# Attention score products of a head pair pinned into an alternating order, upper head first

## The chip, the core and the metric

The kernel runs on one core of one Trainium2 chip. The metric is the device time of one execution in microseconds; the kernel before takes 839.2 us as the median of 3 runs (838.42 to 839.84).

## What is computed

The reference chains three layers over 4 batches of 768 tokens with 8 heads of 48 channels (3072 tokens of 384 channels in all):

```python
state = alpha[:, :, t, :, None] * state + np.einsum('bhd,bhe->bhde', k[:, :, t], v[:, :, t])
y[:, :, t] = np.einsum('bhd,bhde->bhe', q[:, :, t], state)      # gated linear attention
...
h = x @ w_in                                                     # 384 -> 2048
y = (h * (1.0 / (1.0 + np.exp(-h)))) @ w_out                     # 2048 -> 384
...
expert_idx = np.argmax(logits, axis=1)                           # 8 experts, one per token
out[mask] = gate_w[mask, None] * (np.maximum(x[mask] @ w1[e], 0.0) @ w2[e])
```

## The kernel before, in words

**Attention** is done in 24 chunks of 128 tokens (`NCH`; chunk n is tokens c of batch b with c, b = divmod(n, 4)). A chunk handles 8 heads as 4 pairs: a head's 48 channels are padded to 64, so that the lower head of a pair lies on partitions 0 to 63 and the upper one on 64 to 127. The steps of a chunk are written as small functions: `att_A` transposes the decays on TensorE (`transpose4`, L619) and scans them on VectorE (L627), which gives the factors P and R (L632, L634); `att_Bk` and `att_Bq` transpose keys and queries and multiply the factors in (L649, L674); `att_C` (L685 to L702) makes the score products; `att_S` splits the masked scores into two 16-bit parts (L710, L711); `att_KT` scales the keys in place on GpSimd (L724), splits them and sends them through a transposing DMA (L729); `att_D` makes the output y (L758, L765) and splits it (L506); `att_U` multiplies keys and values (L799) and updates the state (L808, L813).

**The score products** are 8 per chunk: for each of 4 pairs p and each head i of it, a 128x128 block of keys times queries in 32-bit floats that contracts the 64 partitions of that head alone. Each product of 32-bit floats appears in the trace as two matmul records and two weight loads, so a chunk has 16 records of L692. The products of the lower heads go to the PSUM bank `sc0`, those of the upper heads to `sc1`. Each bank is copied out as a whole by ScalarE (L697), masked by GpSimd (L698) and used by `att_D`.

**PSUM banks.** `bank` (L390) gives out banks. In the first part of the program they come from all eight; once the blocks run (`turn[0] = None`), every bank that attention asks for, and those of `route`, come from one pool of three (`ps_a`). `att_C` asks for `sc0` first and for `sc1` second, so a score product waits for the reader of whatever lay in its bank before.

**The first feed-forward layer** runs in 8 blocks of 384 tokens: `mm1` (L870, 9 matmuls of 128x384 into `hp`) then SiLU on ScalarE and a split (L877 to L879), and `mm2` (L893, 9 matmuls of 128x392 into three accumulators). While block j runs, the steps of the attention chunks for block j+2 are pumped in between (`pump_j`), and weights of the experts are loaded and split (`pump_w`). At the end of a block `finish` pumps what is missing, and `route` picks the expert of each token and scatters its row. After the last block come `expert1` (L1183) and `expert2` (L1209), tile by tile, to the end.

**What sets the order.** The program is built with a scheduler that plays the instructions through a timeline of its own and fixes the order on each engine by when an instruction is ready there; the order of the source is a wish, not a rule. On the chip each engine then follows that fixed order. `behind` (L480) adds an edge between two instructions of one engine for that scheduler: the one is placed behind the other, without a semaphore between them.

Of the kernel before, what the change touches and what calls it, by code (L numbers as in the profile page):

```python
# [272 lines left out]
def attention_silu_moe_kernel(  # L273
# [14 lines left out]
    nc = tc.nc  # L288
# [83 lines left out]
    if True:  # L372
# [17 lines left out]
        def bank(dims, dtype, name):  # L390
            at = (ps_a, "at")
            wide = [at, at, at, (ps_o, "o0"), (ps_o, "o1"), (ps_o, "o2"), (ps_h, "h"), (ps_h, "h")]
            pool, tag = at if turn[0] is None else wide[turn[0] % 8]
            if turn[0] is not None:
                turn[0] += 1
            return pool.tile(dims, dtype, tag=tag, name=name)
# [83 lines left out]
        def behind(ins, before):  # L480
            tc.add_manual_dep(
                ins.ins, before.ins.name, mybir.DependencyInfo(mybir.DependencyClass.NoSync, mybir.DependencyReason.DATA),
                reason="the first block's tokens come before the weights that it uses last",
            )

        def from64(raw, f, gate=None, first=None):
            r = raw.rearrange("p (n w) -> p n w", w=2)
            lo, hi = r[:, :, 0], r[:, :, 1]
            fi = f.bitcast(I32)
            ins = nc.vector.tensor_scalar(  # L490
                out=fi, in0=hi, scalar1=3, scalar2=0x3FFFFFF8, op0=ALU.logical_shift_left, op1=ALU.bitwise_and
            )
            if gate is not None:
                after(ins, gate)
            if first is not None:
                behind(ins, first)
            nc.vector.scalar_tensor_tensor(
                out=fi, in0=lo, scalar=29, in1=fi, op0=ALU.logical_shift_right, op1=ALU.bitwise_or
            )
            nc.vector.scalar_tensor_tensor(  # L500
                out=fi, in0=hi, scalar=-0x40000000, in1=fi, op0=ALU.bitwise_and, op1=ALU.bitwise_or
            )
# [72 lines left out]
        def load_w1(c, e):  # L575
            st = work[:, F * (e % 2):F * (e % 2 + 1)]
            nc.sync.dma_start(out=st, in_=w1[e, c * 128:(c + 1) * 128, :])
            behind(split(st, SW1, w1s["h"][c][:, e, :], w1s["l"][c][:, e, :]), lead["g"])
            if c == 0:
                nc.vector.tensor_reduce(  # L580
                    out=guard("w1", 2.0 ** -6), in_=st[:, 0:64], axis=AXX, op=ALU.max, apply_absolute_value=True
                )
# [102 lines left out]
        def att_C(n):  # L685
            d = ch[n]
            d["S"] = []
            sc = [bank([128, NPAIR, 128], FP32, f"sc{i}") for i in range(2)]
            for p in range(NPAIR):
                for i in range(2):  # L690
                    r = slice(64 * i, 64 * i + 64)
                    nc.tensor.matmul(  # L692
                        out=sc[i][:, p, :], lhsT=d["K"][r, p, :], rhs=d["Q"][r, p, :], start=True, stop=True
                    )
            for i in range(2):
                s = a2.tile([128, NPAIR, 128], FP32, tag="S", name="S")
                nc.scalar.activation(out=s, in_=sc[i], func=ACTF.Copy, scale=SST if n >= NF else SST * SV)  # L697
                nc.gpsimd.affine_select(  # L698
                    out=s, in_=s, pattern=[[0, NPAIR], [1, 128]], compare_op=ALU.is_ge, fill=0.0, base=0,
                    channel_multiplier=-1,  # L700
                )
                d["S"].append(s)  # L702
# [118 lines left out]
        def att_steps():  # L821
# [10 lines left out]
            for n in range(NCH):  # L832
                more = n + 1 < NCH
                if more:
                    att_A(n + 1)
                    att_load(n + 3, "a")
                yield
                att_C(n)
                yield
                att_S(n)  # L840
# [130 lines left out]
        def weights_a():  # L971
            for c in range(2):
                for e in range(E):
                    load_w1(c, e)
                    yield
# [20 lines left out]
        weights = [weights_a()]  # L996
# [318 lines left out]
        last = lambda t: route(NCH - TPB + t, acc[t])  # L1315
# [91 lines left out]
```

## Time and profile before

| what | value |
|---|---|
| median of 3 runs | 839.2 us |
| the profiled execution | 834.05 us |
| its span, and the mean granted TensorE clock | 832.4 us, 0.974 |
| TensorE busy | 779.0 us, 94% of the span |
| VectorE, ScalarE, GpSimd busy | 500.0, 431.4, 248.2 us |
| score products L692, busy with overlaps counted once | 54.8 us in 384 records |

The profile shows one execution. Its own time, 834.05 us, is 1.65 us more than the span from the first to the last instruction, and 5.15 us less than the median of the runs. "Busy" counts time in which at least one instruction of the group runs, so records that overlap are counted once. The slices divide the span into 40 parts of 20.8 us each.

### The profile page before, as it was taken

The page shows a single profiled execution, that of the slowest core. Times are in us where ns is not written, and L with a number is a line of the kernel's source. Part 1 is how long each engine was busy: PE and PEld are TensorE (multiplying, and loading weights), DVE is VectorE, ACT ScalarE, POOL GpSimd, SP SyncE. Part 2 cuts the span into 40 slices and gives each one's busy share as a digit, 9 for nine tenths or more (in the row PEclk, how much of TensorE's full clock was granted, in tenths as well). Part 3 has the DMA queues.
Part 4 walks back from the last instruction along what each step waited for, and adds up shares of the span by engine and source line. Part 5 has one row for each costly group of instructions (what it writes and reads, how often), then busy time and mean ns, then how long its engine had stood idle before and what let it go on. Part 6 is the DMA issues. An engine that isn't in the chain of part 4 may idle for free. (4 is left out here: it accounts for less than half of the span.)

```text
span 832.4 us, 16583 instructions
## 1 busy us (share of the span) xinstructions
PE 779.0 (94%) x5488; PEld 492.0 (59%) x5488; DVE 500.0 (60%) x1444; ACT 431.4 (52%) x931; POOL 248.2 (30%) x335
## 2 busy tenths in 40 slices
PE   6879799999999999998999988989799999999996
PEld 5756577667667666665657655555344555555553
DVE  7799963767777977786677576466543222222221
ACT  2456664656675846666556575667542222222221
POOL 3342311534453554444222121131343111111111
PEclk9959899999999999999999999999999999999998
DMA  9997132144445454534521345345588666555663
GB/s 188 256 289 201 48 49 48 50 93 80 96 106 118 89 147 100 112 96 86 106 79 47 97 135 159 90 134 153 166 160 188 115 112 121 103 118 120 109 117 61
DMA packets 244028, 98.66 MB, mean 119 GB/s; under 512 B 224969, under 2 KB 233326, under 8 KB 243808
## 3 DMA queue, kind: packets, MB, share of 16 engines
q1 hardware_dynamic: 240288, 86.31, 48.8%
q0 software_dynamic: 3648, 11.18, 3.9%
q8 instruction: 51, 0.84, 0.4%
q14 instruction: 41, 0.34, 0.1%
HBM read 58.40 MB, written 12.36 MB: 85 GB/s over the span
## 5 line engine op out<-in xcount | busy, mean ns | idle before, releaser
L870 PE MATMUL hp<-w2h,wi_h 128*128 128x384 f16 x576 | 146.2, 331 | 7.4 <-ACT w2l L877 5.3
L893 PE MATMUL o<-wo_h,w2l 128*128 128x392 f16 x528 | 147.1, 333 | 6.0 <-DVE wo_h L569 3.6
L1190 DVE SCALAR_TENSOR_TENSOR work<-hp,work 128x512 f16<-128x512 f32 x58 | 39.9, 690 | 121.6 <-ACT work L1189 121.5
L893 PEld LDWEIGHTS <-w2l 128*128 128x128 f16 x792 | 75.5, 98 | 57.9 <-issue 6.9
L870 PEld LDWEIGHTS <-wi_h 128*128 128x128 f16 x768 | 74.0, 98 | 54.7 <-issue 10.1
L1183 PE MATMUL hp<-w1h,xT 128*128 x348 | 103.5, 379 | 2.4 <-DVE work L1190 2.4
L870 PE MATMUL hp<-w2h,wi_l 128*128 128x384 f16 x288 | 94.8, 330 | 0.1
L893 PE MATMUL o<-wo_l,w2l 128*128 128x392 f16 x264 | 87.8, 332 | 0.0
L1183 PEld LDWEIGHTS <-xT 128*128 128x128 f16 x522 | 50.9, 98 | 60.7 <-issue 3.0
L1220 POOL DMA_INDIRECT out_dram<-ob,mt x29 | 28.3, 976 | 176.3 <-ACT ob L1217 171.7
L1189 ACT ACTIVATE work<-hp 128x512 f16<-128x512 f32 x58 | 34.4, 595 | 68.4 <-PE hp L1183 61.6
L893 PE MATMUL o<-wo_h,g 128*128 128x392 f16 x240 | 67.0, 329 | 1.2 <-DVE g L879 1.1
L879 DVE SCALAR_TENSOR_TENSOR w2l<-w2l 128x384 f16<-128x384 f32 x88 | 51.1, 583 | 27.8 <-ACT w2l L878 27.5
L1183 PE MATMUL hp<-w1l,xT 128*128 x174 | 66.0, 379 | 0.0
L877 ACT ACTIVATE w2l<-hp 128x384 f32<-128x384 f32 x88 | 42.4, 483 | 36.0 <-PE hp L870 31.8
L692 PE MATMUL sc<-Q,K 64*128 64x128 f32 x384 | 54.8, 307 | 1.7 <-DVE state L817 1.0
L692 PEld LDWEIGHTS sc<-Q,K 64*128 64x128 f32 x384 | 46.0, 207 | 14.0 <-issue 7.1
L870 PEld LDWEIGHTS <-wi_l 128*128 128x128 f16 x384 | 37.8, 99 | 24.3 <-issue 1.0
L698 POOL TENSOR_SCALAR_AFFINE_SELECT S<-S 128x512 f32<-128x512 f32 x48 | 36.5, 764 | 45.7 <-ACT S L697 45.3
L878 ACT ACTIVATE w2l<-w2l 128x384 f16<-128x384 f32 x88 | 45.7, 521 | 5.8 <-PE o L893 4.1
L870 PE MATMUL hp<-w2l,wi_h 128*128 128x384 f16 x192 | 48.2, 326 | 0.0
L893 PEld LDWEIGHTS <-g 128*128 128x128 f16 x360 | 34.0, 98 | 23.2 <-DVE g L879 2.2
(276 smaller groups left out, 1603.7 us busy)
## 6 DMA issues: line engine op xcount, KB each, us to landing
work<-in_moe_w_dram SPq DMA_DIRECT2D x24, 512.0 KB, 3.8
work<-in_moe_w_dram SPq DMA_DIRECT2D x30, 384.0 KB, 3.5
w1h<-in_moe_w_in_dram SPq DMA_DIRECT2D x6, 768.0 KB, 5.4
nat_a<-in_alpha_dram SPq DMA_DIRECT2D x23, 192.0 KB, 3.2
nat_k<-in_k_dram SPq DMA_DIRECT2D x23, 192.0 KB, 2.8
nat_q<-in_q_dram SPq DMA_DIRECT2D x23, 192.0 KB, 3.2
nat_v<-in_v_dram SPq DMA_DIRECT2D x23, 192.0 KB, 2.9
w1h<-in_moe_w_out_dram SPq DMA_DIRECT2D x5, 768.0 KB, 7.2
```

Source lines behind the costliest of these rows:

```text
L692: nc.tensor.matmul(out=sc[i][:, p, :], lhsT=d["K"][r, p, :], rhs=d["Q"][r, p, :], start=True, stop=True)
L698: nc.gpsimd.affine_select(out=s, in_=s, pattern=[[0, NPAIR], [1, 128]], compare_op=ALU.is_ge, fill=0.0, base=0, channel_multiplier=-1,)
L870: ins = nc.tensor.matmul(out=hp, lhsT=wi[a][f // 2][:, c, (f % 2) * 128:(f % 2 + 1) * 128], rhs=x[:, c, :], start=(n == 0), stop=(n == 3 * ...
L877: nc.scalar.activation(out=g, in_=hp, func=ACTF.Silu, scale=1.0 / (SX * SWI))
L878: nc.scalar.activation(out=gh, in_=g, func=ACTF.Copy, scale=SG)
L879: lead["g"] = nc.vector.scalar_tensor_tensor(out=gl, in0=g, scalar=SG, in1=gh, op0=ALU.mult, op1=ALU.subtract)
L893: nc.tensor.matmul(out=acc[t], lhsT=a[:, ts], rhs=wo[w][f // 2][:, f % 2, :], start=(f == 0 and n == 0), stop=(f == KF - 1 and n == 2),)
L1183: nc.tensor.matmul(out=hp, lhsT=xT[:, a, :], rhs=w1s[w][c][:, bass.ds(d["e"], 1), fs], start=(n == 0), stop=(n == 3 * KD - 1),)
L1189: nc.scalar.activation(out=hs[:, 0], in_=hp, func=ACTF.Relu)
L1190: nc.vector.scalar_tensor_tensor(out=hs[:, 1], in0=hp, scalar=0.0, in1=hs[:, 0], op0=ALU.max, op1=ALU.subtract)
L1220: nc.gpsimd.indirect_dma_start(out=out[:, :], out_offset=bass.IndirectOffsetOnAxis(ap=d["row"], axis=0), in_=ob, in_offset=None, bounds_ch ...
```

## The change

In `att_C` the loop over the two heads is turned round (upper head first), and every score product but the first of a chunk is put behind the one before it with `behind`. The text of the reason in `behind` changes with no effect. Nothing else does: the same products, banks, copies and DMAs.

```diff
             d["S"] = []
             sc = [bank([128, NPAIR, 128], FP32, f"sc{i}") for i in range(2)]
+            prev = None
             for p in range(NPAIR):
-                for i in range(2):
+                for i in (1, 0):
                     r = slice(64 * i, 64 * i + 64)
-                    nc.tensor.matmul(
+                    ins = nc.tensor.matmul(
                         out=sc[i][:, p, :], lhsT=d["K"][r, p, :], rhs=d["Q"][r, p, :], start=True, stop=True
                     )
+                    if prev is not None:
+                        behind(ins, prev)
+                    prev = ins
```

## Rows read from the trace of the kernel before

**Rows 1.** The page: busy time by engine, then TensorE and its clock in 40 slices

```profile
PE 779.0 (94%) x5488; PEld 492.0 (59%) x5488; DVE 500.0 (60%) x1444; ACT 431.4 (52%) x931; POOL 248.2 (30%) x335
...
PE   6879799999999999998999988989799999999996
...
PEclk9959899999999999999999999999999999999998
```

**Rows 2.** Busy time in stretches: length, each engine (instructions), clock, DMA share, GB/s

```profile
42.00:62.00 20.00, 15.35 (x91) 11.04 (x91) 19.38 (x43) 11.93 (x21) 9.15 (x7) 0.50 1.14 285
...
83.00:104.00 21.00, 16.34 (x116) 11.37 (x114) 20.20 (x39) 13.11 (x25) 8.03 (x7) 0.84 0.17 48
...
104.00:464.00 360.00, 353.07 (x2991) 241.78 (x2989) 263.07 (x761) 224.74 (x493) 140.50 (x194) 1.00 0.40 87
464.00:832.00 368.00, 343.31 (x1951) 186.88 (x1948) 144.51 (x479) 152.27 (x341) 68.98 (x83) 0.99 0.58 128
```

**Rows 3.** The same for the score products' line L692 alone: TensorE and weight loads

```profile
5.00:62.00 57.00, 8.89 (x64) 7.63 (x64) 0.79 1.15 257
62.00:104.00 42.00, 3.20 (x16) 2.75 (x16) 0.92 0.47 128
104.00:464.00 360.00, 42.76 (x304) 35.68 (x304) 1.00 0.40 87
```

**Rows 4.** Timeline of TensorE around one chunk: start, length, what, xcount

```profile
258.02 0.49 PE L870 MATMUL hp<-w2l,wi_h 128*128 128x384 f16 x2
258.44 1.16 PE L692 MATMUL sc<-Q,K 64*128 64x128 f32 x8
259.53 0.34 PE L870 MATMUL hp<-w2l,wi_l 128*128 128x384 f16 x1
259.70 0.49 PE L870 MATMUL hp<-w2l,wi_h 128*128 128x384 f16 x2
260.12 1.16 PE L692 MATMUL sc<-Q,K 64*128 64x128 f32 x8
261.21 0.34 PE L870 MATMUL hp<-w2l,wi_l 128*128 128x384 f16 x1
261.38 0.49 PE L870 MATMUL hp<-w2l,wi_h 128*128 128x384 f16 x2
```

**Rows 5.** Timeline of TensorE around the last chunk's score products

```profile
461.43 1.16 PE L692 MATMUL sc<-Q,K 64*128 64x128 f32 x16
462.53 0.34 PE L893 MATMUL o<-wo_h,w2l 128*128 128x392 f16 x1
```

**Rows 6.** Timeline of TensorE around a chunk that follows a route, 228 to 233 us

```profile
228.32 1.16 PE L692 MATMUL sc<-Q,K 64*128 64x128 f32 x8
229.40 0.34 PE L893 MATMUL o<-wo_l,w2l 128*128 128x392 f16 x1
...
230.74 0.49 PE L870 MATMUL hp<-w2l,wi_h 128*128 128x384 f16 x2
231.16 1.16 PE L692 MATMUL sc<-Q,K 64*128 64x128 f32 x8
```

**Rows 7.** Timeline of VectorE ahead of the chunk of rows 4

```profile
257.56 0.53 DVE L506 SCALAR_TENSOR_TENSOR ys<-yp,ys 128x384 f16<-128x384 f32 x1
258.02 0.08 DVE L506 DVE_READ_ACCUMULATOR ys<-yp,ys 128x1 f32 x1
```

**Rows 8.** Waits of TensorE, 62 to 464 us: in total, times, longest

```profile
PE up L799 <- DMA KT<-kd: 4.8, 4, 2.6
...
PE sc L692 <- DVE state L817: 1.0, 1, 1.0
```

**Rows 9.** Line L697, the copies of the scores, 104 to 464 us

```profile
L697 ACT ACTIVATE S<-sc x38: 572/578/598, 116.9 to 463.1; 128x512 f32<-128x512 f32 x38
...
PE sc L692: 7.3, 11
```

**Rows 10.** Line L724, keys scaled in place, 104 to 464 us

```profile
L724 POOL TENSOR_TENSOR K<-K,pend x14: 1037/1041/1529, 161.8 to 391.9; 128x512 f32<-128x512 f32 x14
...
PE sc L692: 2.1, 5
```

**Rows 11.** Timeline of ScalarE around the chunk of rows 4

```profile
260.03 0.58 ACT L697 ACTIVATE S<-sc 128x512 f32<-128x512 f32 x1
...
262.36 0.57 ACT L697 ACTIVATE S<-sc 128x512 f32<-128x512 f32 x1
```

More of the change, by code (lines that the diff above doesn't have):

```diff
@@ L482, in behind @@
                 ins.ins, before.ins.name, mybir.DependencyInfo(mybir.DependencyClass.NoSync, mybir.DependencyReason.DATA),
-                reason="the first block's tokens come before the weights that it uses last",
+                reason="an order within one engine",
             )
```

## The prediction

> **What bounds the kernel now.** I read the page first: TensorE is busy 94% of the span, VectorE 60%, and from the sixth of the 40 slices on nearly every slice of TensorE is full, at the full granted clock [rows 1]. Then the busy time by stretch [rows 2]: from 104 to 464 us, where the feed-forward blocks run with attention pumped in between, TensorE is busy 353.07 of 360 us, VectorE 263.07, ScalarE 224.74, GpSimd 140.50. From 464 us on it is busy 343.31 of 368. Before 104 us it is different: from 42 to 62 us VectorE is busy 19.38 of 20, from 83 to 104 us 20.20 of 21, with TensorE at 15.35 and 16.34. So work taken off TensorE counts in full between 104 and 464 us and hardly at all before.
>
> Next, where the score products stand [rows 3]: 304 of the 384 records of L692 lie between 104 and 464 us, that is 19 of the 24 chunks at 16 records each, and take 42.76 us there.
>
> Then how they stand [rows 4, 5]. In a typical chunk TensorE does 8 records of L692 in 1.16 us, three matmuls of the feed-forward layer, and 8 more records in another 1.16 us. In the last chunk it does all 16 records in the same 1.16 us. The work is equal; the order is not. A product uses 64 of the 128 rows, so two that stand next to each other and use different rows run at the same time; the 16 records in 1.16 us show that. Where one head's four products stand together, they use the same rows and run one after another. That 42.76 = 18 x 2.31 + 1.16 fits 18 chunks of the split kind and one of the paired kind.
>
> **Why they are split.** The loop of before already alternates the heads, but the scheduler places each product when its bank is free. `sc0` is asked for before `sc1`, and both come from the pool of three, so the lower heads' bank comes free first in the scheduler's timeline; it issues those four, fills in with feed-forward matmuls, and issues the four of the upper heads when theirs is free. In chunks behind a route more is filled in [rows 6]: the second run starts at 231.16, 2.84 us after the first. I take the second run to be the upper heads' from the order of the requests; the rows don't name the head.
>
> **The change, part by part.**
>
> *The pinned order.* The first product is now one of the upper heads, whose bank is free last. When it may go, the other seven may go too, and they stand in alternating order. So each of the 18 split chunks should look like the last one.
>
> The cost of a split run: from its start to the start of the next matmul is 259.53 - 258.44 = 1.09 us [rows 4]. It also starts late: of the two matmuls at 259.70, which take 0.49 us together at 0.326 each, the second starts 0.163 later, and one more of them would start at 260.03; the run starts at 260.12, which is 0.09 late. Together 1.18 us a run, 2.36 us a chunk. The paired run costs 462.53 - 461.43 = 1.10 us [rows 5] and one late start, 1.19 us. The difference is 1.17 us a chunk, and 18 x 1.17 = **21.1 us** off TensorE, all of it in the stretch where it is full.
>
> *Upper head first.* Costed at nothing in itself: the work is equal.
>
> *The first part of the program.* The other five chunks' 80 records lie before 104 us and take 8.89 + 3.20 us [rows 3], two of the five in runs that could be shortened further. I cost that at nothing, since VectorE's work is what hides it there (19.38 of 20 and 20.20 of 21 us) [rows 2]. If that cover were gone, pairing would give at most half of what lies there for those two, some 3 us, and that is on the gain's side.
>
> *The added wait.* The lower heads' four products used to go while the upper heads' bank was still held; now all eight stand behind that bank. On TensorE everything placed behind them is queued there, and ScalarE's copies of `sc0` come later by the time between the two runs. Both copies are needed before `att_D` can finish, and the later one isn't later than now, so nobody further on waits longer. What the wait costs TensorE is not in the trace, since it has no such order; bounds: nothing, if the scheduler puts other matmuls in front and the bank is free on the chip when they are done; at most 1.09 us a chunk, the length of the run that used to lie under it, 19.6 us in all. Below nothing it can't be, the wait being new. The rows near it: the split of y that releases a bank of the chunk before ends at 258.10 [rows 7], 0.34 us ahead of the start of even the first run at 258.44 [rows 4]; and a score product is named as having waited for VectorE's state update once in that stretch, for 1.0 us [rows 8]. These lie at the low end, so I take 1.0 us in all.
>
> *Next in line.* With TensorE's 353.07 us down to some 332, VectorE's 263.07 is still 69 us below it, so no other engine becomes the bound on average.
>
> **The sum** against the profiled execution: 834.05 - 21.1 + 1.0 = 813.95 us. The median of the runs shown is 839.2, which is 5.15 us above that execution; I carry the saving over in microseconds: 839.2 - 21.1 + 1.0 = **819 us**.
>
> **A rule that speaks against it.** ScalarE copies each of a chunk's two score banks in 0.578 us, and waited for L692 only 7.3 us over 19 chunks [rows 9]; today the two copies start 2.33 us apart [rows 11]. After the change both banks are full at once and the copies stand one behind the other for 2 x 0.578 = 1.16 us, as long as the paired run itself. The Trainium skill, "TensorEngine Tiling (Array Packing)", section "PSUM Bottleneck", says that packing speeds up the array but not the emptying of PSUM, which can become the bottleneck. By that rule alone nothing would be gained; it makes the second rival below.
>
> **The rivals.**
>
> *The cover is only half replaced.* The scheduler finds too few ready matmuls to place in front of the pinned eight, and TensorE waits for half of the 1.09 us in each chunk: 18 x 0.55 = 9.8 us, which gives 839.2 - 21.1 + 9.8 = 828 us. For it: the first run did lie under the wait. Against it: from the first run's end to the second's start, 0.59 us [rows 4] to 1.76 us [rows 6] of feed-forward matmuls are found to fill in today.
>
> *The copies take over.* If TensorE had to stand for the two copies in each chunk, 18 x 1.16 = 20.9 us come back: 839 us. For it: three banks are few, and two of them are held until copied. Against: ScalarE is busy 224.74 of 360 us [rows 2], and TensorE has feed-forward matmuls to do meanwhile. The same time, 839, results if the change doesn't do what it says, because the scheduler places feed-forward matmuls between the pinned products and so breaks the pairs: an order isn't a neighbourhood.
>
> *Slower: the transposed keys come late.* The in-place scaling of the keys waits for the last score product of the chunk [rows 10], and behind it lie a split, the transposing DMA and then TensorE's L799. TensorE waited for that DMA in 4 of 14 chunks, 4.8 us in all, 2.6 at most [rows 8]. If the new order puts L799 closer behind the scores, this grows. It decides the sign when the 14 waits exceed 21.1 + 4.8 = 25.9 us, 1.85 us each. At 2.6 us in each of the 14: 36.4 - 4.8 = 31.6 us more, 839.2 - 21.1 + 31.6 = 850 us. Against: the chain starts when the scores end, and they end no later than the upper run does now.
>
> **How the numbers follow.** About 0.2%, 1.7 us, is what a measurement of this kernel can tell from no change. The forecast, with the saving kept but for a few microseconds either way (814 to 824 us), 0.78; half replaced, 828 us, 0.12; copies or broken pairs, 839 us, 0.06; late keys, 850 us, 0.04. The range of 8 in 10 is 814 to 829: below, the full 21.1 us with the 3 us of the first part and 1 us of scatter; above, the first rival. Left out are the last two, and a share of the scatter. Faster: 0.78 + 0.12 = 0.90; no difference 0.06; slower 0.04.
>
> **What would show it.** Right: in the timeline of TensorE each chunk after 104 us has one run of 16 records of L692 in about 1.16 us; L692 is busy some 22 us for 304 records where it was 42.76; TensorE's busy time falls by about 21 us, and the stretch from the first route to the last score product by as much; waits of L692 stay at a microsecond or two. The cover is gone if the waits of TensorE name L692 with about 10 us. The copies have taken over if waits name ScalarE's L697. Pairs are broken if L692 still takes over 30 us. The keys come late if the wait for the KT DMA is 20 us or more. The forecast is wrong altogether if L692 is down to 22 us and the time isn't down: then TensorE wasn't what set the end.

## The result and the profile after

The kernel with the change takes 828.98 us as the median of 4 runs (826.74 to 830.09), against 839.52 us (838.42 to 841.26) for the kernel before on the same chip. The ratio is 0.9869, with a 95% interval from 0.9842 to 0.9896: 10.5 us less, and between 8.7 and 13.3. Faster, as forecast; but the forecast was 819 us, and the measured time lies at the very edge of its range of 814 to 829 us, near the time of the first rival.

The page of the kernel after, busy time by engine, then TensorE and its clock in 40 slices (the lines that answer to [rows 1]):

```profile
PE 764.8 (92%) x5488; PEld 476.2 (58%) x5488; DVE 501.3 (61%) x1444; ACT 427.7 (52%) x931; POOL 250.1 (30%) x335
...
PE   6778699999999999999999998999699999999996
...
PEclk9559799999999999999999999999999999999999
```

TensorE is busy 14.2 us less, the other engines as before to within 4 us. Its slices are still nearly all full from the sixth on. The profiled execution after took 828.59 us, near its median; the one before, 834.05, lies some 5 us under its own, so the two traces together show only 5.5 us of the 10.5 (e9 says more on this). Stretches are therefore compared below by what TensorE did in them, not by when they began.

Busy time by stretch, kernel after, columns as in [rows 2]:

```profile
42.00:62.00 20.00, 14.15 (x89) 10.66 (x90) 19.52 (x45) 13.42 (x23) 8.38 (x8) 0.59 1.10 278
83.00:104.00 21.00, 14.19 (x101) 8.87 (x100) 19.09 (x39) 10.90 (x20) 9.03 (x7) 0.76 0.22 57
104.00:464.00 360.00, 350.96 (x3072) 235.28 (x3071) 267.32 (x768) 227.14 (x502) 142.90 (x196) 1.00 0.41 89
```

From 104 to 464 us TensorE idles 360 - 350.96 = 9.0 us where it idled 6.9 [rows 2], and fits more instructions in. Now the score products there, from the view that groups instructions by line (count, busy time, mean ns of one, idle time before):

```profile
L693 PE MATMUL sc<-Q,K 64*128 64x128 f32 x304 | 30.7, 291 | 0.1
```

The same 304 records take 30.7 us where they took 42.76 [rows 3]: **12.1 us off TensorE**, and not the 21.1 of the forecast. The timeline of TensorE around one chunk says why; it answers to [rows 4]:

```profile
262.41 0.33 PE L897 MATMUL o<-wo_l,g 128*128 128x392 f16 x1
262.67 0.49 PE L693 MATMUL sc<-Q,K 64*128 64x128 f32 x2
263.09 0.34 PE L897 MATMUL o<-wo_h,g 128*128 128x392 f16 x1
263.27 0.49 PE L874 MATMUL hp<-w2l,wi_h 128*128 128x384 f16 x2
263.59 0.33 PE L874 MATMUL hp<-w2l,wi_l 128*128 128x384 f16 x1
...
264.24 0.49 PE L874 MATMUL hp<-w2l,wi_h 128*128 128x384 f16 x2
264.66 1.16 PE L693 MATMUL sc<-Q,K 64*128 64x128 f32 x14
265.75 0.34 PE L874 MATMUL hp<-w2l,wi_l 128*128 128x384 f16 x1
```

The chunk has not one run of 16 records but a run of 2 and a run of 14. The first product, by the pinned order the upper head's of pair 0, goes by itself; feed-forward matmuls follow for 1.6 us; then come the other seven, three pairs and one left over. The same two runs stand in all 18 chunks that were split between 104 and 464 us. The lone product costs 263.09 - 262.67 = 0.42 us, the run of 14 costs 265.75 - 264.66 = 1.09, each with a late start of about 0.09 us, worked out as in the prediction: 1.69 us a chunk, where it was 2.36. That is 0.67 us less, and 18 x 0.67 = 12.1 us, the number of the grouped line.

Who waits, kernel after, 104 to 464 us (total, times, longest), first for TensorE, as [rows 8], then for GpSimd:

```profile
PE up L803 <- DMA KT<-kd: 4.7, 5, 1.5
PE o L897 <- DVE w2l L883: 1.7, 3, 0.8
...
POOL K L728 <- PE sc L693: 21.0, 11, 3.2
```

TensorE waits for the transposed keys as long as before (4.7 us against 4.8). GpSimd waits 21.0 us for the last score product before it scales the keys, where it waited 2.1 [rows 10]. In the chunk shown the scaling now stands ahead of both masks (L728 at 265.90 us, L702 from 266.89), where a mask came first before (L698 at 260.69, L724 at 261.36). GpSimd has the room for that, busy 142.90 of 360 us, and TensorE's own idle time grew by 2.1 us in all.

### The profile page after: what moved, and what is told of

The parts are those of the page before. It is cut to its first block, busy times and chain, and to the rows that moved or that the text cites. A ratio compares the mean times of both kernels' runs of the same rounds, so it can differ in the third digit from the quotient of the medians.

```text
span 827.0 us, 16596 instructions
## 1 busy us (share of the span) xinstructions
PE 764.8 (92%) x5488; PEld 476.2 (58%) x5488; DVE 501.3 (61%) x1444; ACT 427.7 (52%) x931; POOL 250.1 (30%) x335
## 5 line engine op out<-in xcount | busy, mean ns | idle before, releaser
L882 ACT ACTIVATE w2l<-w2l 128x384 f16<-128x384 f32 x88 | 45.6, 520 | 4.3 <-PE o L897 2.9
L1213 PEld LDWEIGHTS <-work 128*128 128x128 f16 x336 | 32.9, 98 | 23.3
L1221 ACT ACTIVATE ob<-po,s 128x384 f32<-128x384 f32 x29 | 16.8, 580 | 55.2 <-PE po L1213 35.9
L702 POOL TENSOR_SCALAR_AFFINE_SELECT S<-S 128x512 f32<-128x512 f32 x48 | 31.7, 682 | 44.9 <-ACT S L701 42.2
```

The costliest lines, as they stand in the source:

```text
L702: nc.gpsimd.affine_select(out=s, in_=s, pattern=[[0, NPAIR], [1, 128]], compare_op=ALU.is_ge, fill=0.0, base=0, channel_multiplier=-1,)
L882: nc.scalar.activation(out=gh, in_=g, func=ACTF.Copy, scale=SG)
L1213: nc.tensor.matmul(out=po, lhsT=hT[c // 4][:, (a + c % 4) * 128:(a + c % 4 + 1) * 128], rhs=w2s[w][c][:, bass.ds(d["e"], 1), :], start=(n ...
L1221: nc.scalar.activation(out=ob, in_=po, func=ACTF.Copy, scale=d["fac"], accum_out=guard("finite", 0.0, ALU.not_equal))
```

## The experiments

Every run is compared with runs of the kernel before on the same chip; the column "before, same chip" has their median. The groups ran on different chips, so medians of different groups are better compared by their ratios. "Scores" is the busy time of the score products from 104 to 464 us in the grouped view (for 288 records where it says so, since the last chunk then lies behind 464 us), "idle" is 360 us less the busy time of TensorE in that stretch; both from one profiled execution each.

| kernel | median us | before, same chip | ratio to before, 95% interval | scores us | idle us |
|---|---|---|---|---|---|
| before | 839.52 | 839.52 | 1 | 42.8 | 6.9 |
| after | 828.98 | 839.52 | 0.9869 (0.9842 to 0.9896) | 30.7 | 9.0 |
| e1 lower head first | 833.52 | 838.67 | 0.9941 (0.9909 to 0.9972) | 30.7 | 11.5 |
| e2 turned, unpinned | 843.51 | 838.67 | 1.0070 (1.0044 to 1.0096) | 41.6 (288) | 8.3 |
| e3 both banks | 831.05 | 838.67 | 0.9922 (0.9892 to 0.9953) | 21.4 (288) | 17.7 |
| e4 late only | 826.99 | 838.67 | 0.9873 (0.9843 to 0.9902) | 31.4 | 8.2 |
| e5 unpaired run | 836.35 | 839.92 | 0.9951 (0.9927 to 0.9976) | 30.7 (288) | 13.1 |
| e6 both, late | 831.38 | 839.92 | 0.9898 (0.9861 to 0.9935) | 22.1 (288) | 17.1 |
| e7 turned copies | 847.71 | 839.92 | 1.0092 (1.0058 to 1.0126) | 40.4 (280) | 10.8 |
| e8 held up | 839.94 | 839.92 | 0.9996 (0.9970 to 1.0021) | 23.0 (288) | 18.2 |
| e10 both, VectorE copy | 831.96 | 839.57 | 0.9928 (0.9900 to 0.9956) | 21.4 (288) | 19.4 |
| e11 late, VectorE copy | 839.49 | 839.57 | 1.0006 (0.9985 to 1.0026) | 29.7 (288) | 16.6 |
| e12 fewer pairs | 832.07 | 837.76 | 0.9907 (0.9874 to 0.9940) | 32.6 | 8.7 |

### Which head goes alone, and why: e1 and e2

e1 keeps the pins and puts the lower head first:

```diff
-                for i in (1, 0):
+                for i in (0, 1):
```

> Theory A (a bank of the pool of three goes to whichever product is placed first, so the first product of a chunk, of whichever head, goes alone, and the other seven wait for the second bank): head order doesn't matter. Lower head first with the same pins gives runs of 2 and 14 records again, L692's group busy about 31 us between 104 and 464 us, and the time of the changed kernel, 829 us within 2. Rival B (upper head first is what makes the pairing, since the upper bank is the late one): with the lower head first the gain shrinks or goes, 834 us or more.

TensorE, timeline of one chunk of e1:

```profile
259.94 0.48 PE L693 MATMUL sc<-Q,K 64*128 64x128 f32 x2
260.36 0.34 PE L874 MATMUL hp<-w2l,wi_h 128*128 128x384 f16 x1
...
261.93 1.16 PE L693 MATMUL sc<-Q,K 64*128 64x128 f32 x14
```

The runs are 2 and 14 again, and the scores take the same 30.7 us. So it isn't the upper heads' bank that is late: whichever product is placed first gets the bank that is free first. Theory A is right on the shape. On the time it is off: 833.5 us where 827 to 831 were expected, and a ratio of 0.9941 whose interval lies above that of the change. The score products can't be what differs, since they cost the same. TensorE's idle time is 2.5 us higher (11.5 against 9.0); what else of the new order makes up its distance to the change (4.5 us by the medians, 6 by the ratios) was not settled. So of the change's 10.5 us it isn't shown how much is the pairing's: e1 has the same saving on the score products and gains 5.1 us.

e2 turns the loop and takes the pins out:

```diff
-            prev = None
...
-                    if prev is not None:
-                        behind(ins, prev)
-                    prev = ins
```

> The loop turned round (upper head first) but nothing pinned. Theory A: the scheduler splits the heads as before, now the upper head's four products first: two runs of 8 records, busy 42.8 us between 104 and 464 us, 839.5 us within 2. Rival B (the order of the heads does it): runs of 16 or of 2 and 14 records, 829 us.

TensorE, timeline of one chunk of e2:

```profile
269.23 1.16 PE L692 MATMUL sc<-Q,K 64*128 64x128 f32 x8
270.32 0.34 PE L893 MATMUL o<-wo_h,w2l 128*128 128x392 f16 x1
270.50 0.49 PE L870 MATMUL hp<-w2l,wi_h 128*128 128x384 f16 x2
270.92 1.16 PE L692 MATMUL sc<-Q,K 64*128 64x128 f32 x8
```

Two runs of 8, as in the kernel before: the pins pair the products, not the turning, so Theory A holds on the shape. But the time is 843.5 us, 4.8 us above that of the kernel before on its chip and outside what was expected. ScalarE's timeline of this chunk shows one thing that the turning did:

```profile
272.92 1.06 ACT L697 ACTIVATE S<-sc 128x512 f32<-128x512 f32 x2
```

Both copies come together behind the second run, where they came 2.33 us apart [rows 11], although the first bank is full 1.7 us earlier. e7 tests that.

e7 is e2 with the copies turned as well:

```diff
-            for i in range(2):
+            for i in (1, 0):
                 s = a2.tile([128, NPAIR, 128], FP32, tag="S", name="S")
...
-                d["S"].append(s)
+                d["S"].insert(0, s)
```

> The run with the loop turned and nothing pinned took 843.5 us, with ScalarE's first copy of the scores 1.8 us after the last product instead of 1.0 us ahead of it. Here the copies are turned as well, upper head first. Theory G (the copies are placed in the order of the source, so turning the products alone makes the first copy wait for the last bank, which delays the users): the first copy comes again ahead of the last product and the time goes back to 838 to 840 us. Rival (843.5 us is scatter between orders): it stays at 842 us or above.

The copies stand apart again, and the first begins ahead of the last product (in one chunk at 255.73 us, where the second run starts at 256.23). But it took 847.7 us: Theory G fails on the time. The profiled execution, 854.1 us, is near the slowest of its eight (845.2 to 854.4). Of its other costs the trace names some, the wait for the transposed keys among them (7.1 us against 4.8 from 104 to 464 us), but not one that makes up 8 us. What these two runs do show: three orders in which the heads stand apart from chunk 6 on, with the same score products, take 839.5, 843.5 and 847.7 us (ratios 1, 1.0070 and 1.0092). The order of everything else moves this kernel by several microseconds.

### The missing half: e3, e5, e10 and e8

If the first product also waits until both banks are free, all eight should stand together. e3 adds that to the kernel after, from chunk 6 on:

```diff
+            freed = [x for x in (lead.get(n - 2), lead.get("rk")) if x is not None] if n >= NF else []
...
                     if prev is not None:
                         behind(ins, prev)
+                    else:
+                        for x in freed:
+                            after(ins, x)
...
-            nc.vector.scalar_tensor_tensor(
+            lead["rk"] = nc.vector.scalar_tensor_tensor(
                 out=rk, in0=pr[:, 0:E], scalar=0.0, in1=oh, op0=ALU.add, op1=ALU.mult, accum_out=mf[:, 1:2]
             )
```

> The changed kernel, and from chunk 6 on the first product also waits for the two VectorE instructions that read the banks before (the split of y of the chunk before, and the rank of the last route). Theory A: all 16 records stand in one run of 1.16 us in 18 chunks; a run of 2 costs 0.42 us and a late start 0.09, so 17 x 0.50 = 8.5 us come off: 820.5 us, from 818 to 823, with L692's group busy about 23 us between 104 and 464 us. Rival C (waiting for both banks gives the time back, on TensorE or through ScalarE's copies that then come together): L692's group falls to 23 us but the time stays at 829 us or above, with new waits of TensorE for L692 or by L799.

TensorE, timeline of one chunk of e3; its busy time from 104 to 464 us; and who it waited for there:

```profile
265.16 1.16 PE L694 MATMUL sc<-Q,K 64*128 64x128 f32 x16
266.25 0.34 PE L901 MATMUL o<-wo_h,w2l 128*128 128x392 f16 x1
```

```profile
104.00:464.00 360.00, 342.33 (x3046) 229.01 (x3044) 267.23 (x768) 227.37 (x499) 141.30 (x194) 1.00 0.41 89
```

```profile
PE up L807 <- DMA KT<-kd: 9.4, 8, 2.7
PE yp L773 <- DVE ss L719: 4.1, 7, 1.5
...
PE sc L694 <- DVE ys L506: 0.4, 1, 0.4
```

This is the picture that the prediction drew for the change itself: 16 records in 1.16 us, the scores down to 21.4 us. And it gains nothing: 831.05 us and a ratio of 0.9922, no less than the kernel after. This shape also shows that the banks are what parted the products in the kernel after, since the added waits are for the two readers of the banks. TensorE's idle time rose from 9.0 to 17.7 us. It waits little for the scores' own bank (0.4 us); it waits behind them, for the keys' transposing DMA (9.4 us, 4.7 in the kernel after) and for the split scores (4.1 us, 0.2 in the kernel after). Rival C is right: what full pairing takes off TensorE, it waits out further down the chunk.

Two causes were possible, and e5 was made to part them. It is e3 with only the order within the run changed, so that there are fewer pairs; everything else stands in the same order:

```diff
-            for p in range(NPAIR):
-                for i in (1, 0):
+            for i, p in [(i, p) for i in (1, 0) for p in range(NPAIR)] if n >= NF else [(i, p) for p in range(NPAIR) for i in (1, 0)]:
+                if True:
```

> The kernel of the run that waits for both banks, with the eight products of a chunk in the same place as one run, but the four upper heads first and the four lower heads behind them, so that only the pair at the seam overlaps: 7 steps of 0.22 us where 4 were, 0.67 us more a chunk, 11.5 us over 17 chunks. Everything else stands in the same order. Theory E (the scheduler's timeline costs a product at its time alone, so the fixed order puts too little work between the paired run and its users; what pairing saves there TensorE waits out at L799 and at the products of y): most of the 11.5 us are taken from those waits, idle time of the stretch from 104 to 464 us falls from 17.7 to about 9 us, and the time is 831 to 835 us. Theory F (the waits come from the two banks being copied and masked at the same time, which is as in the other run): the waits stay, and the time is 841 to 844 us.

TensorE, timeline of one chunk of e5, its busy time and its waits from 104 to 464 us:

```profile
264.63 1.71 PE L694 MATMUL sc<-Q,K 64*128 64x128 f32 x16
```

```profile
104.00:464.00 360.00, 346.95 (x3023) 238.00 (x3022) 267.05 (x766) 226.00 (x496) 138.71 (x194) 1.00 0.42 87
```

```profile
PE up L807 <- DMA KT<-kd: 8.3, 8, 2.8
PE yp L773 <- DVE ss L719: 2.6, 4, 1.5
```

The scores take 30.7 us again, 9.3 more than in e3, and idle time falls by 4.6 us, to 13.1. The median rises by 5.3 us, in ratios from 0.9922 to 0.9951, which is 2.4 us, with intervals that overlap; e6 (below), nearly the same kernel as e3 and on e5's chip, is 5.0 us below e5, 4.4 by the ratios. In the two traces, which have the same order on every engine, the stretch from the first route's product to the last one's takes 452.7 us in e3 and 458.2 in e5. So in this order work on the score products counts for about half; the rest comes out of the waits behind them, as Theory E has it. Idle time doesn't fall back to 9 us, though, so part of the waits is there with or without pairs; whether the copies make it, as Theory F has it, is asked in e10. The shares can't be told more closely from two executions, and what the scheduler's timeline charges for a product was not looked at; shown is only that the waits behind the scores take up part of their time.

e10 is e3 with the upper heads' copy on VectorE, so that the two copies run side by side:

```diff
-                nc.scalar.activation(out=s, in_=sc[i], func=ACTF.Copy, scale=SST if n >= NF else SST * SV)
+                if i and n >= NF:
+                    nc.vector.tensor_scalar(out=s, in0=sc[i], scalar1=SST, scalar2=None, op0=ALU.mult)
+                else:
+                    nc.scalar.activation(out=s, in_=sc[i], func=ACTF.Copy, scale=SST if n >= NF else SST * SV)
```

> As the run that waits for both banks, with the upper heads' scores copied out by VectorE in place of ScalarE from chunk 6 on, so that the two copies run side by side. Theory F (part of the waits that pairing brings comes from the two banks being emptied one behind the other): the scores' users are ready some 0.5 us earlier, TensorE's waits at the products of y and at L799 fall from 13.9 us to 8 or less, and the time to 825 to 828 us. Rival (VectorE, busy 267 of 360 us there, is late with the copy and with the rest): 831 us or above.

TensorE's waits of e10, 104 to 464 us:

```profile
PE up L810 <- DMA KT<-kd: 4.8, 5, 1.6
PE sc L694 <- DVE ys L506: 2.4, 3, 1.2
PE ptr L619 <- DVE R L634: 2.2, 3, 0.9
PE yp L776 <- DVE ss L722: 1.8, 4, 0.8
PE yp L776 <- ACT ss L721: 1.6, 3, 0.8
```

The wait for the transposed keys is halved, so the copies on ScalarE may have had a share in it: in the chunk of e3, ScalarE begins the keys' split (L734) only at 268.69 us, after both copies, though the keys were scaled by 267.45. But VectorE now keeps TensorE waiting elsewhere (2.4 and 2.2 us), and idle time is 19.4 us. At 832.0 us the rival holds: the wait moved.

e8 starts from e6 (below) and places L799's products one step later:

```diff
-                    nc.tensor.matmul(
+                    ins = nc.tensor.matmul(
...
+                    if p == 0 and m == 0:
+                        behind(ins, lead["mm"])
...
+                for _ in range(1 if n >= NF else 0):
+                    yield
                 att_U(n)
...
+                    lead["mm"] = ins
```

(`lead["mm"]` is the last product that `mm2` issued.)

> As the run with both banks from chunk 6 on, and L799's products placed one step of the loop later and behind the last product of the feed-forward layer issued by then, so that more work stands between the scores and L799. Theory E: the wait of TensorE for the transposed keys falls from 9.4 us to 4 us or less, and the time falls to 822 to 826 us, unless the attention chunks now run late for their blocks. Rival: the wait only moves to the products that need the updated state, 829 us or above.

The wait for the keys fell from 9.3 us in e6 to 5.2, yet idle time is 18.2 us and the time 839.9 us, so this gives back all that the pairs save. The rival is right on the time. Where it has the wait move to isn't shown: TensorE's largest waits beside the keys' are 2.3 us at L619 and 1.9 at the feed-forward layer (L882), not at the products that need the updated state.

### The other parts: e4, e6, e11, e12 and e9

e4 pins and turns from chunk 6 on alone:

```diff
-                for i in (1, 0):
+                for i in (1, 0) if n >= NF else (0, 1):
...
-                    if prev is not None:
+                    if prev is not None and n >= NF:
```

> The change from chunk 6 on alone; chunks 0 to 5 in the order of before, unpinned. In the profile of the changed kernel the chunks 3 to 5 start 2.0 to 2.7 us later than before. Theory D (the pins cost that time at the start): 826 to 827 us. Rival (the shift is scatter of one execution, or of the new order as a whole; chunk 5 loses its pairing too): 829 to 830 us.

827.0 us, and a ratio of 0.9873, against 0.9869 for the whole change: no difference that can be measured. The pins in the first part show neither cost nor gain, and the traces speak against Theory D. Up to 157 us e4 has the same order on TensorE as the kernel before, yet its chunk 5 starts at 118.0 us, as late as in the kernel after (117.2; kernel before 115.1). In e6, e8 and e11, whose first part is the same again, it starts at 116.8 to 118.0. So that shift isn't the pins'. The granted clock from 21 to 42 us was 0.59 to 0.63 in these four, 0.90 in the trace of before. e4 has the lowest median of all, but not a better kernel by these intervals.

e6 is e3 with the same restriction.

> Both banks waited for and pinned from chunk 6 on alone, chunks 0 to 5 as before. If the pins at the start cost 2 us, as the run with late pins alone may show against the change: 829 us against 831. If that was scatter: 831 or more.

831.4 us, ratio 0.9898: as e3 within the intervals. e11 is e4 with the copy on VectorE that e10 has.

> The pins from chunk 6 on alone (827.0 us), with the upper heads' copy on VectorE. Theory F: 823 to 826 us. Rival as in the run before: 827 us or above.

839.5 us, so Theory F fails here: the whole gain is gone, with the scores still at 29.7 us, idle time at 16.6 us and the wait for the transposed keys at 9.8 us.

e12 takes one pair out of the change itself, with everything else in its place:

```diff
+            alone = [(1, 0), (0, 0), (0, 1), (0, 2), (1, 1), (1, 2), (1, 3), (0, 3)]
-            for p in range(NPAIR):
-                for i in (1, 0):
+            for i, p in alone if n >= NF else [(i, p) for p in range(NPAIR) for i in (1, 0)]:
+                if True:
```

> The changed kernel with the order within the run of 14 records turned from chunk 6 on (lower heads of pairs 0 to 2, upper heads of pairs 1 to 3, lower head of pair 3), so that two pairs overlap where three did; every other instruction of every engine stands where it stands in the changed kernel. One step of 0.22 us more in 17 chunks, 3.8 us. If work of TensorE counts in full in the changed kernel (few of its waits lie behind the scores: idle 9.0 us of 336.7): 832 to 834 us, idle about the same. Theory E as in the run that waits for both banks (about half of it is taken from waits behind the scores): 830 to 832 us, idle 2 us less. If the gain of the change were its order alone: 829 us, with the 3.8 us wholly taken from waits.

TensorE, timeline of one chunk of e12:

```profile
266.59 1.26 PE L694 MATMUL sc<-Q,K 64*128 64x128 f32 x14
```

The run takes 1.26 us where 1.16 stood, not 1.38: 0.10 us is lost and not the 0.22 of a whole product, since records and not whole products overlap. The scores take 32.6 us, 1.9 more. The median is 3.1 us higher, but on another chip and with intervals that overlap, so this run is inconclusive on how much of the work counts; idle time (8.7 us against 9.0) shows none of it taken from waits.

e9 is the kernel before, profiled once more.

> The kernel before, profiled once more, since its profiled execution (834.05 us) lies 5 us under its median. If that was scatter of single executions, this one is 838 to 841 us, and its score products take the same time (42.8 us between 104 and 464 us), so the difference sits in waits or in the clock of the part behind the attention.

835.72 us: again below the median (839.57 in that group), with scores at 42.8 us. It was not within the 838 to 841 us expected. The recorded clocks say something of where its 4 us lie. The mean granted clock of the execution was 0.977 here and 0.974 in the first profiled execution. Of the 22 runs in e9's group the five at 0.974 or more took 834.4 to 840.0 us, four of them under 836.2; the other 17, at 0.960 to 0.971, took 836.8 to 845.6. Part of the difference shows early: chunk 5 starts at 114.6 us here and at 115.1 in the first trace, and at 116.8 or later in the four kernels with the same first part (e4). So both traces of the kernel before are of quick executions, and a comparison with them shows less of the gain than the medians do; what raised the clock is not shown.

## Why the prediction was right or wrong

- **What bounds the kernel.** TensorE was full between 104 and 464 us, and a cut there did show: 12.1 us less work, 10.5 us less time (8.7 to 13.3). That these two agree is no proof that the work counted in full, since orders with the same score products differ by several microseconds (e1 against the change, e2 and e7 against the kernel before). In the traces the stretch from the first route's product to the last one's fell from 461.6 to 452.6 us with the change (462.0 in e9), and to 459.7 in e1 with the same products' time. What can be said: the seven kernels that pin a chunk's eight products from chunk 6 on and leave the copies and L799 alone (the change, e1, e3 to e6, e12) are all faster than the kernel before, at 827.0 to 836.4 us, and the three that don't pin them and keep the heads apart are at 839.5 to 847.7.
- **Why they were split.** Right that the products wait for banks: two runs of 8 stand in e2 too, with the heads turned, and in e3 waiting for both banks' readers puts all eight together. That the lower heads' bank is the early one in itself was wrong (next point).
- **The pinned order.** This step failed. "The first product is now one of the upper heads, whose bank is free last": it isn't. The first product placed takes the bank that is free first, whichever head it is (e1), goes alone, and the other seven wait for the second bank. The term of 1.17 us a chunk measured 0.67; the sum of 21.1 us measured 12.1. That 828.98 us still lies inside the range of 814 to 829 is luck: the upper end was drawn for another cause.
- **The first part of the program**, costed at nothing: no difference shown (e4).
- **The added wait**, 1.0 us: TensorE's idle time from 104 to 464 us rose by 2.1 us. The size was near, in one execution each; the place was not: 0.1 us lies at L693. The 1.0 us of [rows 8] was no near row either: that wait lies before 104 us, and none of L692 is listed behind it. The sentence "nobody further on waits longer" was wrong. GpSimd waited 18.9 us longer for the last product (21.0 against 2.1), though in the change this didn't reach TensorE's wait for the keys, and e3, where all eight stand together, has 8.7 us more idle time on TensorE than the change: the wait for the keys at L807 is 4.7 us longer and that for the split scores at L773 3.9.
- **"So no other engine becomes the bound on average"**: true of the averages and of no use. VectorE has 93 us to spare in that stretch, and TensorE still waits for single results of the chunk's chain, each in its turn, because its order is fixed.
- **The rivals.** The first gave the time, 828 us, by another way: the cover was not what failed, the pairing was half. Broken pairs came true in part: one product of eight is parted from the rest. The copies didn't take over in the change. In e3 TensorE waits for the split scores and the transposed keys; the copies may have a share in both, but in e10 the copies side by side gained nothing. The late keys didn't come in the change (4.7 us), but they did in e3 (9.4 us), where they are the largest wait.
- **A rule that speaks against it.** In the change both copies do stand one behind the other, and it still gained 10.5 us. In e3 the gain of further pairing was lost behind the array; the longest wait there was for the keys' DMA (9.4 us), halved when one copy left ScalarE (e10), with no gain in time. The Trainium skill, "TensorEngine Tiling (Array Packing)", section "PSUM Bottleneck", says that tiling doesn't speed up the emptying of PSUM, and that after a speedup of 4x this may become the bottleneck. The trace of e3 agrees in so far as the loss came behind the array; that the emptying was the limit no run here shows.
- **What would show it.** The sign that was named for broken pairs was L692 over 30 us; it came at 30.7. The signs for right failed: two runs and not one of 16, 30.7 us and not 22, TensorE's busy time down by 14.2 and not 21. From the first route's product to the end of the last score product the traces have 313.0 us before and 309.0 after, 4.0 less and not 21.

## What to carry to other kernels

Before counting on products that overlap when they stand next to each other, ask what each waits for: an order pinned within an engine leaves gaps wherever one of them has a wait of its own, and here the bank that was free first went to whichever product was placed first. Work taken off the fullest engine shortens the kernel only as far as what it does next is ready: with an order fixed beforehand, the time saved in front of a chain of other engines can turn into a wait at the chain's end, as in e3. Where any new order moves the time by several microseconds, as here, hold a gain against a second order with the same work before giving it to the mechanism.

## What the runs showed of the hardware

Two 32-bit products on different rows overlap by record, and not only where whole products stand next to each other. With the upper and the lower four apart, the 16 records took 1.71 us (e5), and with two seams instead of an alternating order the 14 took 1.26 us (e12), 0.1 us longer than alternating; counted by whole products, both should have lost 0.22 us for each pair given up, 0.67 and 0.22 us, and they lost 0.55 and 0.10.

The starts of the single records say how. Records on the same rows start 0.11 us apart, but for 0.21 after the first. In e5 a second row of such starts begins 0.55 us into the run, 6 ns behind the fifth record, although eight records are placed ahead of it; in e12 it begins at 0.33 us, 6 ns behind the third, with six placed ahead. So in both, in every chunk from 6 to 22, three records are overtaken by one on other rows. Which head a record belongs to is read from the spacing and from the long first record of each row (0.37 us where the others take 0.27); the trace doesn't name it.
